# Attention over a sliding window, then a gelu layer: one pair's values and denominators in one 128-column product, and three blocks of the next first product begun ahead

## The chip, the core and the metric

The kernel runs on one core of a Trainium2 chip. A core has a matrix engine (TensorE, here PE, with its weight loads shown as PEld), a vector engine (DVE), a scalar engine for activation functions (ACT), a general engine (POOL, GpSimd) and a queue engine (SP). They run side by side and wait for each other through semaphores. DMAs are issued from SP, ACT and POOL. Matmuls write PSUM, eight banks of 512 float32 columns on 128 partitions; everything else lives in SBUF. The metric is the device time of one execution in microseconds; 311.24 us is the median of five runs before the change.

## The reference

Eight batches of 576 positions with 8 heads of 64 elements go through attention in which a position sees only those within 32 of it. The result, 4608 tokens of 512 elements, goes through a feed-forward layer with a gelu in its tanh form.

```python
scores = scale * np.matmul(q, k.transpose(0, 1, 3, 2))          # q, k, v: (8, 8, 576, 64)
mask = np.abs(pos[:, None] - pos[None, :]) <= 32
attn = softmax of the masked scores
x = np.matmul(attn, v) as (8 * 576, 8 * 64)
out = gelu_tanh(x @ w_in) @ w_out                                # (512, 2048) and (2048, 512)
```

## The kernel before

**Tiles and batches.** The feed-forward layer works on nine tiles `t` of 512 tokens. While PE does tile `t`, pieces of the attention of batch `b = t + 1` are put between its matmuls; attention writes its output, transposed and in float16, into a ring `xT` of 1536 tokens from which the next tile reads. A batch of 576 positions doesn't fit the ring evenly, so in some batches a write wraps around and becomes two instructions.

**Attention.** Heads are taken in pairs: a pair's two heads lie in the two halves of the 128 partitions. Groups 0 to 3 are the four pairs over the first 480 positions of a batch (512 in batch 0); group 4 is the rest of all pairs and is weighed in the next tile, where the plan calls it -1. A group goes through five steps. `score` (L345): matmuls of keys and queries into the two-bank tiles `S0` and `S1`, and ACT's Exp of them. `mask` (L364): DVE sets to zero what lies outside the window. `weigh` (L373): for each of four pieces of keys and each of the two heads, PE multiplies 64 columns of V by the exponentials into bank `O` (tile `ps_o`), and 64 columns of ones by the same exponentials into bank `D` (`ps_d`), which gives the denominators on 64 partitions for each head. `invert` (L398): ACT takes Ln of the denominators (L401) and Exp of minus that (L402). `spread` (L405): DVE multiplies the two and writes `xT` (L411).

**The feed-forward layer.** `ffn_in` (L429) makes a block of 128 rows of the hidden layer: four matmuls of 512 columns, one for each pair of heads (so the fourth reads what pair 3 has written), and then a gelu on ACT (L454). There are 16 blocks to a tile. The second product (`ffn_out`, L525) is done for two halves of rows and columns with seven products of sums instead of eight, each 16 matmuls of 256 columns (L544); DVE makes the sums (L490) and gathers the results, the last in `ffn_last` (L577, L582). A product accumulates in bank x0 or x1, in turns; blocks of the first product go through x0, x1 and `D`.

**What sets the order.** Each engine runs its instructions in the order in which the kernel writes them. The dictionary `PLAN` (L45) says ahead of which of the 112 matmuls of `ffn_out` a step of attention stands: `v3`, the weighing of pair 3, at 97 and `x3`, its spread, at 112, after the last. Then come `ffn_last`, and the first three matmuls of two blocks of the next tile (`begun`, L763); the next tile opens with their fourth matmuls, which wait for `x3`. ACT loads a table of functions when it goes from Exp and Ln to gelu and back (L87). After the begun blocks DVE casts the queries and keys of the next batch (`cast_and_turn`, L302), SP's queue transposes them by DMA (L313, L319), and later loads those of the batch after (`load_qk`, L152). `load_v` (L167) loads V for batches 2 to 7 from POOL's queue with five DMAs that also cast; batches 0 and 1 are loaded by SP and cast by POOL and ACT (`cast_v`, `cast_vt`).

Of the kernel before, what the change touches and what calls it, by code (L numbers as in the profile page):

```python
# [54 lines left out]
           [(t4, fc) for t4 in (2, 3) for fc in range(16)])  # L55


RING = 1536


@with_exitstack
def kernel(
# [47 lines left out]
    kinds = [MAIN[0], MAIN[1], TAIL, MAIN_0[1], TAIL_0]  # L110
    masks = [const.tile([128, width(ps)], FP16, name=f"mask{i}") for i, ps in enumerate(kinds)]
    KTs = [const.tile([128, NPAIR, 640], FP16, name=f"KT{i}") for i in range(2)]
    Vs = [const.tile([128, 5, H, 64], FP16, name=f"V{i}") for i in range(2)]
    w_in16 = big.tile([128, 4, DF], FP16, name="w_in16")
    w_out16 = big.tile([128, NF, DM], FP16, name="w_out16")
    xT = big.tile([128, NPAIR, RING], FP16, name="xT")
# [1 line left out]
    raws = {}  # L118

    def load_early(b):  # L120


        qr = rawp.tile([128, H, 256], FP32, name="qr")
        kr = rawp.tile([128, H, 256], FP32, name="kr")
        tr = tailp.tile([128, H, 64], FP32, name="tr", tag="tr")
        raws[b] = [qr, kr, tr]

        def qk(h0):
            for src, dst in ((q, qr), (k, kr)):
                nc.sync.dma_start(  # L130
                    dst[:, h0:h0 + 2, :],
                    src[b, h0:h0 + 2, 0:512, :].rearrange("h (p j) d -> p h (j d)", j=4))

        def vs(*heads):
            for h in heads:
                if h == 0:
                    raws[b].append(stage.tile([128, 4, H, 64], FP32, name="vr", tag="stage"))
                    raws[b].append(tailp.tile([128, H, 64], FP32, name="vt"))
# [116 lines left out]

    def cast_vt(b):
        n = 128 if b else 64
        (nc.gpsimd.tensor_copy if b else nc.scalar.copy)(Vs[b % 2][0:n, 4, :, :], raws[b][4][0:n])

    def cast_v(b, pr):  # L260
        vr = raws[b][3]
        hs = slice(2 * pr, 2 * pr + 2)
        nc.gpsimd.tensor_copy(Vs[b % 2][:, 0:4, hs, :], vr[:, :, hs, :])  # L263


    def cast_tails(b, eng):
        t16 = hp.tile([128, H, 64], FP16, name="t16")
        eng.tensor_copy(t16, raws[b][2])
        halfs[b].append(t16)

# [31 lines left out]
    def cast_and_turn(b):  # L302
        cast_open(b)
        q16, k16 = halfs[b]
        qr, kr, qt, kt = raws[b]
        qt16 = hp.tile([16, NPAIR, 4, 2, 64], FP16, name="qt16")
        kt16 = hp.tile([64, NPAIR, 2, 64], FP16, name="kt16")
        def queries(src, dst, p0, p1):
            for pr in range(NPAIR):
                nc.vector.tensor_copy(  # L310
                    dst[:, pr, :, :, :].rearrange("p j h d -> p h j d"),
                    src[:, 2 * pr:2 * pr + 2, :].rearrange("p h (j d) -> p h j d", j=4))
# [51 lines left out]
    def mask(b, g, hfs=(0, 1)):  # L364
        for hf, (m, prs, pieces) in enumerate(halves_of(b, g)):
            if hf not in hfs:
# [3 lines left out]
                pe, pe, m.rearrange("p (o w) -> p o w", o=1).broadcast_to(list(pe.shape)),  # L370
                op=ALU.mult)

    def weigh(b, g, other=False):  # L373

        pes = groups.pop((b, g))
# [5 lines left out]
        for i, (hf, pr, k0, c, p0, p1, off) in enumerate(todo):  # L381
            q0, n = (0, cut(b)) if g < 4 else (cut(b), 144 - cut(b))
            at = 0 if g < 4 else pr * 4 * n
            for w, bk in ((0, o), (1, d)):
                for h in range(2):
                    r0 = 64 * h
                    nc.tensor.matmul(  # L387
                        bk[r0:r0 + 64, at:at + 4 * n].rearrange(
                            "d (j p) -> d j p", j=4)[:, :, p0 - q0:p1 - q0],
                        V[:, c, 2 * pr + h, :] if w == 0 else ones,  # L390
                        pes[hf][:, h, off:off + 4 * (p1 - p0)].rearrange("k (j p) -> k j p", j=4),
                        start=(i == 0), stop=(i == len(todo) - 1), skip_group_check=True)
        return o, d
# [1 line left out]
    def size(b, g):  # L395
        return 4 * cut(b) if g < 4 else 4 * NPAIR * (144 - cut(b))

    def invert(b, g, d):  # L398
        n = size(b, g)
        lt = ap_.tile([128, 512], FP32, name="lt")  # L400
        nc.scalar.activation(lt[:, 0:n], d[:, 0:n], AF.Ln)  # L401
        nc.scalar.activation(lt[:, 0:n], lt[:, 0:n], AF.Exp, scale=-1.0)  # L402
        return lt

    def spread(b, g, o, lt):  # L405
        n = size(b, g)
        if g < 4:
            pos, done = b * S % RING, 0
            while done < n:
                e = min(n - done, RING - pos)  # L410
                nc.vector.tensor_tensor(xT[:, g, pos:pos + e], o[:, done:done + e],  # L411
                                        lt[:, done:done + e], op=ALU.mult)
                done, pos = done + e, (pos + e) % RING
        else:
            pos = (b * S + 4 * cut(b)) % RING
# [13 lines left out]
    def ffn_in(t, n, d0=0, d1=4, then=True):  # L429
# [3 lines left out]
        if d0 == 0:  # L433
            if t == 0 and 2 <= fc < 6:
                if fc % 2 == 0:
                    phs["S"] = psS.tile([128, 2, 512], FP32, name="ph2", tag=f"S{fc // 2 - 1}")
                phs[fc] = phs["S"][:, fc % 2, :]
            else:
                if t:
                    i = (first(t), 2, 1 - first(t))[n % 3] if n < NF - 1 else 2  # L440
                else:
                    i = fc if fc < 2 else (fc - 4) % 3
                phs[fc] = bank(i) if i < 2 else psO.tile([128, 512], FP32, name="ph", tag="D")
        ph = phs[fc]
        for dc in range(d0, d1):
            nc.tensor.matmul(ph, w_in16[:, dc, fc * 128:fc * 128 + 128],  # L446
# [11 lines left out]
    def first(t):  # L458

        return (t + 1) % 2  # L460

    wino = {}

# [61 lines left out]
    def ffn_out(t, i):  # L525
# [90 lines left out]

    def weighed(g):
        o, d = weigh(0, g, other=(g % 2 == 0))
        ods[g] = (o, invert(0, g, d))

    ods = {}
    score(0, 0)
# [74 lines left out]
    for t in range(NT):  # L697
        b = t + 1
        att = b < B
        if t:  # L700
            for fc in range(begun):
                ffn_in(t, fc, 3, 4)
            if att and b > 1:
                cast_and_turn(b)
            for fc in range(begun, NF):
# [11 lines left out]
        for i in range(113 if t else 65):  # L717
            for act in plan.get(i, "").split():
# [22 lines left out]
                elif kind == "v":  # L741
                    bb, gg = group(g)
                    o, d = weigh(bb, gg)
                    ods[g] = (o, invert(bb, gg, d))
# [49 lines left out]
```

## Time and profile before

| | |
|---|---|
| median of five runs | 311.24 us (310.76 to 311.39) |
| the profiled execution's own time | 311.24 us |
| its span in the profile | 309.4 us |
| PE matmuls busy | 298.1 us (96%) |
| PE weight loads busy | 187.4 us (61%) |
| DVE, ACT, POOL busy | 198.9, 199.9, 103.2 us |
| granted TensorE clock | full in all slices |
| tiles 2, 3, 5 (first matmul to first matmul of the next) | 31.81, 31.80, 31.80 us |
| tile 4 | 31.87 us |

A row of the order of time gives the start in us, the duration, the engine, the line of the kernel, the operation, output and input by the program's names, shapes, how many were merged ("x15"), and in brackets the idle time before it and what ended it. Matmuls overlap: one with 256 columns is shown as 0.27 us long, while the next starts 0.11 us later. So the pace of PE is read from the starts. "PE A <- DVE B: 0.4, 1, 0.4" in the table of waits reads: PE's A waited for DVE's B, 0.4 us in total, once, 0.4 us at the longest. The page's chain is the work that ended last, followed back to the start, as shares of the span.

### The profile page before, as it was taken

Reading aid. Unit: us, or ns where it says so; the run is one execution under the profiler, and the core shown is the slowest. Engines: PE = TensorE matmul, PEld = TensorE weight load, DVE = VectorE, ACT = ScalarE, POOL = GpSimd, SP = SyncE. Lnnn points to the kernel's source line nnn. Section 1 sums busy time; section 2 is a strip of 40 time slices with the busy share of each in tenths; the row PEclk is TensorE's granted clock in tenths of the full one; section 3 lists DMA queues with packets and bytes.
Section 4 is the critical chain, followed back from the end, with each engine's and each line's share of the span. In section 5 each row is a group of like instructions: output and inputs, shape, how many; then the busy total and the mean of one; then the engine's idle time right before and its main releaser. Section 6 shows DMA issues by size and latency. Waiting matters only on the chain.

```text
span 309.4 us, 6731 instructions
## 1 busy us (share of the span) xinstructions
PE 298.1 (96%) x2643; PEld 187.4 (61%) x2643; DVE 198.9 (64%) x453; ACT 199.9 (65%) x315; POOL 103.2 (33%) x158
## 2 busy tenths in 40 slices
PE   7879999999999999999999999999999999999993
PEld 2453545445784588548854785478647864784583
DVE  5763587868968476947784678666866643632451
ACT  1776576577677786778676776677768676706600
POOL 3656455093019110921093108510710061006000
PEclk9999999999999999999999999999999999999999
DMA  6999998999987999899779985999391022004013
GB/s 189 261 354 368 374 340 188 310 180 145 225 179 179 129 199 166 148 169 230 137 157 146 262 120 133 162 247 140 91 169 34 2 70 68 2 0 136 2 37 100
DMA packets 120061, 50.64 MB, mean 164 GB/s; under 512 B 101327, under 2 KB 113359, under 8 KB 120030
## 3 DMA queue, kind: packets, MB, share of 16 engines
q1 hardware_dynamic: 84329, 37.50, 57.7%
q0 software_dynamic: 34768, 11.54, 33.3%
q10 hardware_dynamic: 933, 1.18, 1.1%
q8 instruction: 20, 0.33, 0.5%
q14 instruction: 11, 0.09, 0.1%
HBM read 37.62 MB, written 9.44 MB: 152 GB/s over the span
## 4 chain that ended last, share of the span: by engine, by line
PE 76%; DMA 9%; SPq 7%; DVE 5%; POOL 1%; issue 1%; ACT 0%; DVEq 0%; POOLq 0%
PE mm L544 30%; PE mm L446 20%; PE ph L446 12%; PE ps_o L387 4%; DMA wst<-in_moe_w_in_dram 4%; PE ps_s L354 3%; PE ps_d L387 3%; DMA KT<-k 3%; DMA kr<-in_k_dram 2%; SPq L162 2%; PE mm L515 2%; SPq L130 2%; SPq L139 1%; POOL w_in L190 1%; SPq L181 1%
## 5 line engine op out<-in xcount | busy, mean ns | idle before, releaser
L446 PEld LDWEIGHTS <-w_in 128*128 128x128 f16 x576 | 56.0, 98 | 66.6 <-POOL w_in L190 1.7
L446 PE MATMUL mm<-xT,w_in 128*128 128x512 f16 x352 | 86.3, 379 | 0.2 <-DVE xT L411 0.2
L506 POOL DMA_DIRECT2D out_dram<-y x77 | 45.3, 595 | 115.4 <-DVE y L573 114.7
L454 ACT ACTIVATE gT<-mm 128x512 f16<-128x512 f32 x88 | 52.4, 599 | 37.2 <-PE mm L446 37.2
L446 PE MATMUL ph<-xT,w_in 128*128 128x512 f16 x224 | 58.8, 379 | 0.6 <-POOL w_in L190 0.6
L490 DVE TENSOR_TENSOR s<-gT 128x512 f16<-128x512 f16 x64 | 26.9, 420 | 42.0 <-ACT gT L454 42.0
L544 PEld LDWEIGHTS <-s 128*128 128x128 f16 x512 | 48.6, 98 | 7.5
L360 ACT ACTIVATE pe<-ps_s 128x704 f16<-128x704 f32 x64 | 43.3, 727 | 9.1 <-PE ps_s L354 8.3
L544 PE MATMUL mm<-t,s 128*128 128x256 f16 x376 | 45.7, 273 | 0.0
L401 ACT ACTIVATE lt<-ps_d 128x480 f32<-128x480 f32 (+3 forms) x40 | 22.2, 556 | 30.9 <-PE ps_d L387 30.8
L454 ACT ACTIVATE gT<-ph 128x512 f16<-128x512 f32 x56 | 33.0, 600 | 13.0 <-PE ph L446 12.9
L544 PEld LDWEIGHTS <-gT 128*128 128x128 f16 x384 | 36.0, 98 | 7.3
L369 DVE TENSOR_TENSOR pe<-pe,mask 128x704 f16<-128x704 f16 x64 | 31.8, 533 | 1.7 <-ACT pe L360 1.6
L544 PE MATMUL mm<-w_out,gT 128*128 128x256 f16 x256 | 32.8, 273 | 0.0
L411 DVE TENSOR_TENSOR xT<-ps_o,lt 128x480 f16<-128x480 f32 (+5 forms) x38 | 20.2, 549 | 12.7 <-ACT lt L402 12.7
L387 PEld LDWEIGHTS <-V 128*64 128x64 f16 x336 | 17.9, 109 | 11.3 <-issue 5.4
L402 ACT ACTIVATE lt<-lt 128x480 f32<-128x480 f32 (+3 forms) x40 | 23.5, 588 | 1.3
L387 PE MATMUL ps_o<-pe,V 128*64 128x160 f16 (+2 forms) x244 | 21.7, 241 | 1.1 <-POOL V L263 0.8
L87 ACT ACT_TABLE_LOAD x17 | 21.8, 1283 | 1.1 <-PEq L778 0.8
L387 PE MATMUL ps_d<-pe,ones 128*64 128x192 f16 (+2 forms) x264 | 22.3, 235 | 0.0
L170 POOL DMA_DIRECT2D V<-in_v_dram x24 | 22.0, 942 | 0.0
L354 PE MATMUL ps_s<-QT,KT 64*128 64x192 f16 (+5 forms) x336 | 17.9, 227 | 1.1 <-DVE KT L290 1.1
(77 smaller groups left out, 297.6 us busy)
## 6 DMA issues: line engine op xcount, KB each, us to landing
kr<-in_k_dram SPq DMA_DIRECT2D x32, 256.0 KB, 7.2
qr<-in_q_dram SPq DMA_DIRECT2D x6, 1024.0 KB, 7.5
V<-in_v_dram POOLq DMA_DIRECT2D x30, 128.0 KB, 8.1
wst<-in_moe_w_in_dram SPq DMA_DIRECT2D x3, 1024.0 KB, 8.9
wst<-in_moe_w_out_dram SPq DMA_DIRECT2D x3, 1024.0 KB
qr<-in_q_dram SPq DMA_DIRECT2D x8, 256.0 KB
vr<-in_v_dram SPq DMA_DIRECT2D x16, 128.0 KB, 7.5
out_dram<-y POOLq DMA_DIRECT2D x24, 48.0 KB, 2.4
```

What stands on the lines that cost most here:

```text
L170: nc.gpsimd.dma_start(V[:, c, :, :], v[b, :, 128 * c:128 * c + 128, :].rearrange("h p d -> p h d"))
L354: nc.tensor.matmul(ps[:, h, off:off + 4 * n].rearrange("k (j p) -> k j p", j=4), KTs[b % 2][r0:r0 + 64, pr, k0:k0 + 128], QTs[b][r0:r0 + 6 ...
L360: nc.scalar.activation(pe, ps[:, :, 0:w], AF.Exp, scale=SCALE)
L369: nc.vector.tensor_tensor(pe, pe, m.rearrange("p (o w) -> p o w", o=1).broadcast_to(list(pe.shape)), op=ALU.mult)
L387: nc.tensor.matmul(bk[r0:r0 + 64, at:at + 4 * n].rearrange("d (j p) -> d j p", j=4)[:, :, p0 - q0:p1 - q0], V[:, c, 2 * pr + h, :] if w == ...
L401: nc.scalar.activation(lt[:, 0:n], d[:, 0:n], AF.Ln)
L402: nc.scalar.activation(lt[:, 0:n], lt[:, 0:n], AF.Exp, scale=-1.0)
L446: nc.tensor.matmul(ph, w_in16[:, dc, fc * 128:fc * 128 + 128], xT[:, dc, t * 512 % RING:t * 512 % RING + 512], start=(dc == 0), stop=(dc = ...
L454: nc.scalar.activation(gTs[t][:, fc, :], phs[fc], AF.Gelu_apprx_tanh)
L490: nc.vector.tensor_tensor(dst, x, y, op=op)
L506: (eng or turn_about[0] if t == NT - 1 else eng or nc.gpsimd).dma_start(out_v[b, j, q0 + p:q0 + p + e, cols], yo[m:m + e, cols])
L544: nc.tensor.matmul(pys["apart"][:, 0:256] if apart else py[:, blk, :], lhsT, wino[w][:, f, :], start=(new and i % (8 if one else 16) == 0) ...
```

## The change

In batches 2 to 7 the weighing of pair 3 is done with 128 columns at a time. V gets a ninth place between the last two heads, filled with ones once, so that head 6 and the ones, and the ones and head 7, lie side by side. One matmul of [V6, ones] then gives in bank `O` the weighted values of head 6 on partitions 0 to 63 and its denominators on 64 to 127; one of [ones, V7] gives in bank `D` the denominators of head 7 on 0 to 63 and its values on 64 to 127. Eight matmuls with full-width weights take the place of sixteen with half-width ones. `invert` needs two Ln instructions, each on 64 partitions and from one half of the partitions to the other, and `spread` two multiplications for one, the second reading `D`. Head 7 moves to another place, so `load_v` has seven DMAs for five and the casts of the early batches are split or strided.

Three blocks of the next tile are begun ahead instead of two, the second and third in the two-bank tile `S0` of the scores. The rotation of banks in `ffn_in` and `ffn_out` is the same in every tile now and no longer swaps. Two pairs of small tiles share a buffer in SBUF (`vt` with `qt`, `t16` with `kt16`).

```diff
+FUSED = (3,)
-    Vs = [const.tile([128, 5, H, 64], FP16, name=f"V{i}") for i in range(2)]
+    Vs = [const.tile([128, 5, H + 1, 64], FP16, name=f"V{i}") for i in range(2)]
...
-        qt = tailp.tile([16, H, 256], FP32, name="qt")
+        qt = tailp.tile([16, H, 256], FP32, name="qt", tag="vt")
...
     def load_v(b):
         V = Vs[b % 2]
-        for c in range(4):
-            nc.gpsimd.dma_start(V[:, c, :, :],
-                                v[b, :, 128 * c:128 * c + 128, :].rearrange("h p d -> p h d"))
-        nc.gpsimd.dma_start(V[:, 4, :, :], v[b, :, 448:576, :].rearrange("h p d -> p h d"))
+        for c, k0 in enumerate((0, 128, 256, 384, 448)):
+            nc.gpsimd.dma_start(V[:, c, 0:7, :],
+                                v[b, 0:7, k0:k0 + 128, :].rearrange("h p d -> p h d"))
+        nc.gpsimd.dma_start(V[:, 0:4, 8, :], v[b, 7, 0:512, :].rearrange("(c p) d -> p c d", p=128))
+        nc.gpsimd.dma_start(V[:, 4, 8, :], v[b, 7, 448:576, :])
...
     def cast_vt(b):
-        (nc.gpsimd.tensor_copy if b else nc.scalar.copy)(Vs[b % 2][0:n, 4, :, :], raws[b][4][0:n])
+        copy = nc.gpsimd.tensor_copy if b else nc.scalar.copy
+        copy(Vs[b % 2][0:n, 4, 0:7, :], raws[b][4][0:n, 0:7])
+        copy(Vs[b % 2][0:n, 4, 8, :], raws[b][4][0:n, 7])
...
+    def fused(b, g):
+        return b > 1 and g in FUSED
...
+            if fused(b, g):
+                for h, bk in enumerate((o, d)):
+                    nc.tensor.matmul(
+                        bk[:, 0:4 * n].rearrange("d (j p) -> d j p", j=4)[:, :, p0:p1],
+                        V[:, c, 2 * pr + h:2 * pr + h + 2, :],
+                        pes[hf][:, h, off:off + 4 * (p1 - p0)].rearrange("k (j p) -> k j p", j=4),
+                        start=(i == 0), stop=(i == len(todo) - 1), skip_group_check=True)
+                continue
             for w, bk in ((0, o), (1, d)):
...
-        nc.scalar.activation(lt[:, 0:n], d[:, 0:n], AF.Ln)
+        if fused(b, g):
+            nc.scalar.activation(lt[0:64, 0:n], o[64:128, 0:n], AF.Ln)
+            nc.scalar.activation(lt[64:128, 0:n], d[0:64, 0:n], AF.Ln)
+        else:
+            nc.scalar.activation(lt[:, 0:n], d[:, 0:n], AF.Ln)
         nc.scalar.activation(lt[:, 0:n], lt[:, 0:n], AF.Exp, scale=-1.0)
...
-                nc.vector.tensor_tensor(xT[:, g, pos:pos + e], o[:, done:done + e],
-                                        lt[:, done:done + e], op=ALU.mult)
+                for bk, rows in ((o, slice(0, 64)), (d, slice(64, 128))) if fused(b, g) else \
+                        ((o, slice(0, 128)),):
+                    nc.vector.tensor_tensor(xT[rows, g, pos:pos + e], bk[rows, done:done + e],
+                                            lt[rows, done:done + e], op=ALU.mult)
...
-                    i = (first(t), 2, 1 - first(t))[n % 3] if n < NF - 1 else 2
+                    i = 3 if n in (1, 2) else 0 if n == 0 else (2, 1, 0)[n % 3]
...
+                if i == 3 and n == 1:
+                    phs["S"] = psS.tile([128, 2, 512], FP32, name="ph3", tag="S0")
...
-            pys[n % 2] = bank((first(t) + n) % 2)
+            pys[n % 2] = bank((1 + n) % 2)
...
             for fc in range(begun):
-                ffn_in(t, fc, 3, 4)
+                ffn_in(t, fc, 3, 4, then=False)
+            for fc in range(begun):
+                gelu(t, fc)
...
+                        if t == 1:
+                            nc.gpsimd.memset(Vs[1][:, :, 7, :], 1.0)
                         load_v(b + 1)
...
+            nc.gpsimd.memset(Vs[0][:, :, 7, :], 1.0)
             load_v(2)
...
-        begun = 2 if att else 0
+        begun = 3 if att else 0
```

More of the change, by code (lines that the diff above doesn't have):

```diff
@@ L137, in vs @@
                     raws[b].append(stage.tile([128, 4, H, 64], FP32, name="vr", tag="stage"))
-                    raws[b].append(tailp.tile([128, H, 64], FP32, name="vt"))
+                    raws[b].append(tailp.tile([128, H, 64], FP32, name="vt", tag="vt"))
                 nc.sync.dma_start(raws[b][3][:, :, h, :],
@@ L262, in cast_v @@
         hs = slice(2 * pr, 2 * pr + 2)
-        nc.gpsimd.tensor_copy(Vs[b % 2][:, 0:4, hs, :], vr[:, :, hs, :])
+        nc.gpsimd.tensor_copy(
+            Vs[b % 2][:, 0:4, 2 * pr:2 * pr + 3:2 if pr == 3 else 1, :][:, :, 0:2, :], vr[:, :, hs, :])
     def cast_tails(b, eng):
-        t16 = hp.tile([128, H, 64], FP16, name="t16")
+        t16 = hp.tile([128, H, 64], FP16, name="t16", tag="t16")
         eng.tensor_copy(t16, raws[b][2])
@@ L306, in cast_and_turn @@
         qt16 = hp.tile([16, NPAIR, 4, 2, 64], FP16, name="qt16")
-        kt16 = hp.tile([64, NPAIR, 2, 64], FP16, name="kt16")
+        kt16 = hp.tile([64, NPAIR, 2, 64], FP16, name="kt16", tag="t16")
         def queries(src, dst, p0, p1):
@@ L389, in weigh @@
                             "d (j p) -> d j p", j=4)[:, :, p0 - q0:p1 - q0],
-                        V[:, c, 2 * pr + h, :] if w == 0 else ones,
+                        V[:, c, 2 * pr + h + (pr == 3 and h), :] if w == 0 else ones,
                         pes[hf][:, h, off:off + 4 * (p1 - p0)].rearrange("k (j p) -> k j p", j=4),
@@ L396, in size, with invert, spread @@
         return 4 * cut(b) if g < 4 else 4 * NPAIR * (144 - cut(b))
-    def invert(b, g, d):
+    def invert(b, g, o, d):
         n = size(b, g)
         lt = ap_.tile([128, 512], FP32, name="lt")
-        nc.scalar.activation(lt[:, 0:n], d[:, 0:n], AF.Ln)
+        if fused(b, g):
[3 more added lines that the diff above has]
+            nc.scalar.activation(lt[:, 0:n], d[:, 0:n], AF.Ln)
         nc.scalar.activation(lt[:, 0:n], lt[:, 0:n], AF.Exp, scale=-1.0)
-        return lt
-    def spread(b, g, o, lt):
+        return lt, d
+    def spread(b, g, o, lt, d):
         n = size(b, g)
@@ L439, in ffn_in @@
                 if t:
-                    i = (first(t), 2, 1 - first(t))[n % 3] if n < NF - 1 else 2
+                    i = 3 if n in (1, 2) else 0 if n == 0 else (2, 1, 0)[n % 3]
                 else:
                     i = fc if fc < 2 else (fc - 4) % 3
-                phs[fc] = bank(i) if i < 2 else psO.tile([128, 512], FP32, name="ph", tag="D")
+                if i == 3 and n == 1:
+                    phs["S"] = psS.tile([128, 2, 512], FP32, name="ph3", tag="S0")
+                phs[fc] = bank(i) if i < 2 else phs["S"][:, n - 1, :] if i == 3 else \
+                    psO.tile([128, 512], FP32, name="ph", tag="D")
         ph = phs[fc]
@@ L456, in gelu @@
             sums(t, n // 4)
-    def first(t):
-        return (t + 1) % 2
     wino = {}
@@ L618, in weighed @@
         o, d = weigh(0, g, other=(g % 2 == 0))
-        ods[g] = (o, invert(0, g, d))
+        ods[g] = (o, *invert(0, g, o, d))
     ods = {}
@@ L743 @@
                     o, d = weigh(bb, gg)
-                    ods[g] = (o, invert(bb, gg, d))
+                    ods[g] = (o, *invert(bb, gg, o, d))
                     if t and g < 0 and b + 1 < B:
+                        if t == 1:
+                            nc.gpsimd.memset(Vs[1][:, :, 7, :], 1.0)
                         load_v(b + 1)
```

## The prediction

> **What bounds the kernel now.** I read the page first (engines, chain), then the table of who waited for whom, then the order of time around one tile's end, engine by engine.
>
> ```profile
> PE 298.1 (96%) x2643; PEld 187.4 (61%) x2643; DVE 198.9 (64%) x453; ACT 199.9 (65%) x315; POOL 103.2 (33%) x158
> PE 76%; DMA 9%; SPq 7%; DVE 5%; POOL 1%; issue 1%; ACT 0%; DVEq 0%; POOLq 0%
> ```
>
> PE is busy throughout and carries the chain; DMA and SP's queue are its opening, before the weights have come. After 60 us PE waits once (second batch's tile):
>
> ```profile
> PE ps_o L387 <- DVE xT L411: 0.4, 1, 0.4
> ```
>
> So what counts is the spacing of PE's instructions, not their busy time. Here is the end of tile 2 (PE, then DVE, then ACT, each in order of time: start, us, what):
>
> ```profile
> 121.95 0.27 PE L544 MATMUL mm<-w_out,s 128*128 128x256 f16 x1
> 122.16 0.26 PE L387 MATMUL ps_o<-pe,V 128*64 128x160 f16 x2
> 122.25 0.24 PE L387 MATMUL ps_d<-pe,ones 128*64 128x160 f16 x2
> 122.32 0.25 PE L387 MATMUL ps_o<-pe,V 128*64 128x192 f16 x2
> ...
> 122.70 0.22 PE L387 MATMUL ps_d<-pe,ones 128*64 128x128 f16 x2
> 122.86 1.81 PE L544 MATMUL mm<-w_out,s 128*128 128x256 f16 x15
> 124.51 0.81 PE L446 MATMUL mm<-xT,w_in 128*128 128x512 f16 x3
> 125.15 0.81 PE L446 MATMUL ph<-xT,w_in 128*128 128x512 f16 x3
> 125.80 0.38 PE L446 MATMUL mm<-xT,w_in 128*128 128x512 f16 x1
> ```
>
> ```profile
> 121.38 0.66 DVE L411 TENSOR_TENSOR xT<-ps_o,lt 128x480 f16<-128x480 f32 x1 [0.53 <-ACT lt L402]
> ...
> 124.21 0.66 DVE L411 TENSOR_TENSOR xT<-ps_o,lt 128x480 f16<-128x480 f32 x1 [0.90 <-ACT lt L402]
> 124.78 0.74 DVE L582 TENSOR_TENSOR y<-mm,y 128x256 f32<-128x256 f32 x2
> 125.44 1.45 DVE L310 CAST q<-qr 128x512 f16<-128x512 f32 x4
> ```
>
> ```profile
> 122.97 0.57 ACT L401 ACTIVATE lt<-ps_d 128x480 f32<-128x480 f32 x1 [0.93 <-PE ps_d L387]
> 123.57 0.60 ACT L402 ACTIVATE lt<-lt 128x480 f32<-128x480 f32 x1
> 124.19 1.28 ACT L87 ACT_TABLE_LOAD   x1
> ```
>
> The reader should see two things. The two 64-column matmuls of a "x2" row run side by side: 160 columns advance PE by 0.07 us, 192 by 0.08, 128 by 0.055. And the group pays at its edges: L544 matmuls stand 0.11 apart (15 in 1.65), yet the first L387 starts 0.21 after its forerunner, and the next L544 0.16 after the last pair instead of 0.055. Each edge costs 0.10. The six tiles that the change touches (1 to 6) show 0.90 or 0.91 from that last L544 to the next.
>
> **The change, part by part.** *The fused product (tiles 1 to 6).* Eight full-width matmuls replace eight side-by-side pairs and stream the same columns: 2 x (0.07 + 0.08 + 0.08 + 0.055), 0.58 with unrounded spacings. Nothing shows V's 128 columns loaded for a matmul this short, so the nearest row is the tail transposes, which load 128 columns for 128 moving ones:
>
> ```profile
> 55.56 0.39 PE L274 MATMUL pt<-idn,t 128*128 128x128 f16 x4
> 55.79 0.38 PE L515 MATMUL mm<-w_out,gT 128*128 128x512 f16 x1
> ```
>
> Four in 0.23, 0.056 each, no edge before or after. I take it: same width, same length. The other bound is the 0.11 spacing of the L544 stream, 8 x 0.11 = 0.88.
>
> The Trainium skill, "TensorE: Matmul & The Clock Gate", section "LDWEIGHTS (loading the stationary operand)", speaks against the change: it gives columns/1.2 ns, 107 ns for 128 columns. By that the eight loads would need 0.85, and as an estimate the six tiles would lose 0.6 us in all where I count a gain; the transposes' 0.056 decides against it here.
>
> The edge at the exit goes: 0.10. The one at the entrance goes only as far as DVE allows, since the group writes the bank that the spread of pair 2 reads. That spread ends at 121.38 + 0.66 = 122.04; DVE to PE takes 0.06 (the wait above: DVE's two rows at 83.37 end 84.08, PE starts at 84.14). So the group starts at 122.10, not 122.06. In tiles 1 and 4 the ring wraps and pair 2's spread is two instructions (0.72): it ends at 90.30 and 185.77, and entry gains nothing (90.35, 185.82 now). From last L544 to next: 0.15 + 0.58 = 0.73 in four tiles, 0.20 + 0.58 = 0.78 in two. Gain: 4 x 0.18 + 2 x 0.13 = 0.98 us.
>
> *The longer way to xT, and the third block.* Now: L401 0.57, L402 0.60, spread 0.66, end 124.87, with PE wanting xT at 125.80: 0.87 spare with the 0.06. After: the group starts at 122.10, its last matmul 0.53 later, takes 0.22, ACT starts 0.05 after (122.70 + 0.22 to 122.97): 122.90. The second Ln follows by 0.49 (gelus start at 126.22 and 126.71) and ends at 123.96; Exp to 124.59, first spread from 124.63, second 0.57 behind (124.21 to 124.78), end 125.86. No row shows half the partitions, or an ACT output on other partitions than its input; I take the full-width times, with nothing and twice as bounds. PE wants it at 122.10 + 0.58 + 1.65 + nine matmuls of 0.215 (six took 1.29) = 126.27. Spare: 0.35; 0.15 if the pairs don't overlap (0.60 and 0.66). Without the third block, 0.65 less, it would be late. The block itself adds no matmul. Its two banks of scores were last read by ACT at 122.04 (121.25 + 0.79) and are wanted from 125.16; bank 1, wanted by block 4 at 127.8, is freed by L582 at about 126.5. The table load moves to 124.6, ends 125.9, ahead of the first gelu at 126.7. The first product of each tile now always takes bank 1, last read by block 13's gelu, some 0.9 earlier. Cost nothing.
>
> *DVE later.* L582 and the casts behind it start 1.0 later (125.77 for 124.78). Behind them: the q transposes on SP's queue, then the four key transposes, then the next loads; on POOL the stores and V loads. Landing events in tile 2 put keys of pairs 1 and 2 at 108.71 and 111.96, PE wanting them at 110.20 and 113.36: spare 1.5 and 1.4, of which 1.07 goes for DVE (two split spreads precede it there) and 0.12 since PE comes earlier. Left: 0.2 to 0.3. Tile 3's least is 2.0. No cost taken; the bound is about 1 us should the landings stretch.
>
> *V loads.* Seven POOL issues for five, 2 x 0.94 = 1.9 us a tile. The last three wait for the tail group (109.01 in tile 2), after which POOL idles 13.25 us for DVE's y; first use is a tile later. The waits of these issues on earlier stores of the same queue have long been met. The two fills of ones (0.26 for 192 columns; bounds 0.2 to 0.6) delay V of batch 2 from 62.56; it is wanted at 80.43. But that traffic meets batch 2's key transposes, whose first arrival PE's weight load only just meets (0.2 waited at 75.00): -0.2 to +0.6 there, taken as 0.
>
> *The split casts.* ACT's V tail (0.61 at 12.34) becomes two instructions, up to 0.6 more, followed by 0.34 idle and hidden by the wait for w_in until 26.7; POOL's (0.62 at 52.76) is followed by 1.25 idle. SP's qt load now waits for the latter: done by 54.0 at worst, while SP reaches it at 59.74; kt stands behind it. Nothing.
>
> Sum: 311.24 - 0.98 = 310.26, against the profiled execution's own 311.24 (span 309.4, 1.8 outside); that is also the median. I say 310.3.
>
> **The rivals.** *Eaten by loads (same).* Keys or V traffic late in tiles 1 and 2 give back 0.4 to 1.2: 310.7 to 311.5. For: 0.2 to 0.3 spare is thin and DMA is at 9 tenths there. Against: V chunks carry seven heads, not eight. *Loads of weights set the pace (slower).* At 0.11 a matmul the span is 0.15 + 0.88 = 1.03 in four tiles and 1.08 in two: +0.5 + 0.35 = +0.8, 312.1. The gain is gone at 0.093 a matmul, and from 0.106 it is slower; only the transposes speak against it. *xT late (slower).* With the way to xT 0.35 + e longer than counted, PE stands e in each of six tiles; beyond e = 0.16 the gain is gone, and if each half took the full extra again (0.57 + 0.66, e = 0.9) it would be 315.6. *More (faster).* Entry gain everywhere and tile 1's 0.4 wait gone: 309.7. *The change doesn't do what it says (same).* If the full-width group has edges of 0.10 too, it lasts 0.21 + 0.58 + 0.10 = 0.89 for 0.91: 311.1. The transposes' missing edges speak against it.
>
> **How the numbers follow.** Likeliest, 309.9 to 310.6: 0.58. Eaten, or edges that stay: 0.21. Slower rivals: 0.16 together. More: 0.05. A change of 0.2%, 0.62 us, is what a measurement can tell: faster below 310.62, 0.63; same to 311.86, 0.21; slower 0.16. The range leaves out the worst of both ends: 309.7 to 311.7.
>
> **What would show it.** Right: the fused group takes 0.58, the next L544 starts 0.06 after its last matmul, tiles 2, 3, 5 and 6 last 31.62 instead of 31.80. PE waits for xT at L446's fourth slice, or idle time ended by KT in tile 2, would show the rivals; matmuls 0.11 apart in the group the weight loads. I am wrong if half-partition ACT or DVE work costs more than whole, or if landings in tile 2 stretch.

## The result, and the profile after

The changed kernel takes 311.23 us (median of 53 runs, 310.4 to 314.32); the kernel before, run beside it, 311.81 us (median of 95, 310.57 to 314.93; the 311.24 named at the start is the median of five of these). The ratio is 0.9981 with a 95% interval of 0.9972 to 0.999: a gain of about 0.6 us, at least 0.3, where the forecast's sum was 0.98 (a ratio of 0.9969, just outside the interval). The 311.23 lies inside the stated range, but 0.97 above the 310.26 of the sum: 0.57 of this is the base (311.24 in five runs, 311.81 in 95), 0.40 is gain that is missing. The forecast took 0.2% as the least that a measurement can tell; the middle of the interval, 0.19%, is just under it, and the interval reaches to both sides.

The page of the changed kernel, engines and chain, in the order of the lines shown of before:

```profile
PE 296.8 (96%) x2595; PEld 187.3 (61%) x2595; DVE 204.2 (66%) x461; ACT 201.9 (65%) x322; POOL 113.0 (37%) x173
...
PE 85%; SPq 4%; DMA 4%; DVE 3%; POOL 1%; issue 1%; ACT 0%; POOLq 0%
```

PE still carries the chain; it has 48 matmuls less (8 in each of six tiles). The table of waits has the wait of before in tile 1, and one after 60 us that is new:

```profile
PE ph L476 <- ACT gT L484: 0.7, 1, 0.7
...
PE ps_o L408 <- DVE xT L438: 0.4, 1, 0.4
```

The end of tile 2 in order of time (PE, then DVE, then ACT; start, duration, what). The lines of the code have moved: L476 is the first product (L446 before), L570 the second (L544), L399 the fused product, L423 and L424 its two Ln, L427 the Exp, L438 the spread, L484 the gelu.

```profile
121.93 0.27 PE L570 MATMUL mm<-w_out,s 128*128 128x256 f16 x1
122.07 0.23 PE L399 MATMUL ps_o<-pe,V 128*128 128x160 f16 x1
...
122.59 0.22 PE L399 MATMUL ps_d<-pe,V 128*128 128x128 f16 x1
122.64 1.80 PE L570 MATMUL mm<-w_out,s 128*128 128x256 f16 x15
124.28 0.81 PE L476 MATMUL mm<-xT,w_in 128*128 128x512 f16 x3
124.93 1.46 PE L476 MATMUL ph<-xT,w_in 128*128 128x512 f16 x6
126.22 0.38 PE L476 MATMUL mm<-xT,w_in 128*128 128x512 f16 x1
```

```profile
124.61 0.65 DVE L438 TENSOR_TENSOR xT<-ps_o,lt 64x480 f16<-64x480 f32 x1 [1.32 <-ACT lt L427]
125.29 0.66 DVE L438 TENSOR_TENSOR xT<-ps_d,lt 64x480 f16<-64x480 f32 x1
...
126.66 1.45 DVE L318 CAST q<-qr 128x512 f16<-128x512 f32 x4
```

```profile
122.79 0.57 ACT L423 ACTIVATE lt<-ps_o 64x480 f32<-64x480 f32 x1 [0.77 <-PE ps_o L399]
123.38 0.56 ACT L424 ACTIVATE lt<-ps_d 64x480 f32<-64x480 f32 x1
123.97 0.60 ACT L427 ACTIVATE lt<-lt 128x480 f32<-128x480 f32 x1
```

The group lasts 0.57 (122.07 to 122.64), and from the last L570 before it to the next there are 0.71 for 0.91 before. PE wants the finished xT at 126.22 and doesn't stand: the second spread ends at 125.95.

**Where the gain went.** A tile is measured from its first L476 (L446) to that of the next. Tiles 1 to 7 (tile 0 is the opening) took 32.27, 31.80, 31.80, 31.87, 31.80, 31.80 and 26.66 us before, and 32.22, 31.60, 31.60, 31.74, 31.60, 31.60 and 26.66 after. So 0.05, 0.20, 0.20, 0.13, 0.20 and 0.20, together 0.98: the whole forecast gain is there when the last tile begins. Then this, in the order of time of PE and of ACT:

```profile
277.49 1.03 PE L476 MATMUL mm<-xT,w_in 128*128 128x512 f16 x4
278.35 1.03 PE L476 MATMUL ph<-xT,w_in 128*128 128x512 f16 x4
280.06 1.89 PE L476 MATMUL ph<-xT,w_in 128*128 128x512 f16 x8 [0.69 <-ACT gT L484]
```

```profile
278.55 0.60 ACT L484 ACTIVATE gT<-mm 128x512 f16<-128x512 f32 x1 [9.46 <-PE mm L476]
279.41 0.60 ACT L484 ACTIVATE gT<-ph 128x512 f16<-128x512 f32 x1 [0.27 <-PE ph L476]
```

and the same place of the kernel before:

```profile
278.45 1.03 PE L446 MATMUL mm<-xT,w_in 128*128 128x512 f16 x4
279.31 1.03 PE L446 MATMUL ph<-xT,w_in 128*128 128x512 f16 x4
280.17 1.89 PE L446 MATMUL mm<-xT,w_in 128*128 128x512 f16 x8
```

Before, a block starts every 0.86. After, block 2 starts 1.71 behind block 1, 0.85 late, and only when block 1's gelu (279.41 + 0.60) is done. Blocks 1 and 2 lie in the two halves of `S0`, the buffer (a tile of PSUM, in the kernel's word) that otherwise holds scores. In tiles 1 to 7 all three first blocks are begun ahead and their gelus are written behind all of them. Tile 8 isn't begun ahead (`begun` is 0 once no attention is left), so each block's gelu stands behind it in the order of writing, and block 2's matmuls, which write the buffer that the gelu reads, wait for it, though the two use different halves. The first two experiments test this.

A second measure is needed for what follows, since the opening (before tile 1) differs by 1.3 us between two profiles of the changed kernel, and by 2 us among all twelve profiles, as the last section shows. From the first matmul of tile 1 to the end of the span the kernel before takes 248.99 us, the changed one 248.75, and 248.75 again in a second profile. In this measure the change is worth 0.24: 0.98, less 0.85 between the first matmul of tile 8 and the start of the last one of the second product (26.78 for 25.93), plus 0.10 gained behind that, in the stores (4.94 for 5.05). The 0.10 needn't be the change's: all the other kernels show 4.93 to 5.00 there, and of the kernel before there is one profile only.

### The profile page after: what moved, and what is told of

Its sections match the earlier page's. It is cut to its first block, busy times and chain, and to the rows that moved or that the text cites. A ratio compares the mean times of both kernels' runs of the same rounds, so it can differ in the third digit from the quotient of the medians.

```text
span 309.2 us, 6674 instructions
## 1 busy us (share of the span) xinstructions
PE 296.8 (96%) x2595; PEld 187.3 (61%) x2595; DVE 204.2 (66%) x461; ACT 201.9 (65%) x322; POOL 113.0 (37%) x173
## 4 chain that ended last, share of the span: by engine, by line
PE 85%; SPq 4%; DMA 4%; DVE 3%; POOL 1%; issue 1%; ACT 0%; POOLq 0%
PE mm L570 30%; PE mm L476 21%; PE ph L476 16%; PE mm L541 5%; PE ps_s L362 4%; PE ps_o L408 4%; DMA wst<-in_moe_w_in_dram 4%; PE ps_d L408 2%; SPq L134 2%; SPq L143 1%; POOL w_in L195 1%; SPq L186 1%; PE ps_o L399 1%; DVE t L506 1%; PE py L570 1%
## 5 line engine op out<-in xcount | busy, mean ns | idle before, releaser
L476 PEld LDWEIGHTS <-w_in 128*128 128x128 f16 x576 | 56.0, 98 | 67.3 <-POOL w_in L195 1.6
L476 PE MATMUL mm<-xT,w_in 128*128 128x512 f16 x320 | 78.0, 379 | 0.1
L484 ACT ACTIVATE gT<-mm 128x512 f16<-128x512 f32 x80 | 47.6, 599 | 36.3 <-PE mm L476 35.6
L476 PE MATMUL ph<-xT,w_in 128*128 128x512 f16 x256 | 64.6, 379 | 1.2 <-ACT gT L484 0.7
L570 PEld LDWEIGHTS <-s 128*128 128x128 f16 x512 | 48.8, 98 | 7.0
L570 PE MATMUL mm<-t,s 128*128 128x256 f16 x376 | 45.8, 273 | 0.0
L484 ACT ACTIVATE gT<-ph 128x512 f16<-128x512 f32 x64 | 36.3, 602 | 12.3 <-PE ph L476 12.1
L570 PEld LDWEIGHTS <-gT 128*128 128x128 f16 x384 | 36.0, 98 | 7.4
L174 POOL DMA_DIRECT2D V<-in_v_dram x30 | 29.1, 984 | 22.8 <-PE ps_d L408 14.3
L426 ACT ACTIVATE lt<-ps_d 128x480 f32<-128x480 f32 (+3 forms) x34 | 18.8, 553 | 25.3 <-PE ps_d L408 25.2
L570 PE MATMUL mm<-w_out,gT 128*128 128x256 f16 x256 | 32.8, 273 | 0.0
L438 DVE TENSOR_TENSOR xT<-ps_o,lt 128x480 f16<-128x480 f32 (+10 forms) x38 | 20.3, 548 | 15.9 <-ACT lt L427 15.7
L427 ACT ACTIVATE lt<-lt 128x480 f32<-128x480 f32 (+3 forms) x40 | 23.5, 587 | 1.3
L408 PEld LDWEIGHTS <-V 128*64 128x64 f16 x288 | 15.4, 109 | 9.9 <-issue 4.4
L408 PE MATMUL ps_o<-pe,V 128*64 128x160 f16 (+2 forms) x196 | 17.5, 241 | 1.0 <-DVE pe L377 0.4
L408 PE MATMUL ps_d<-pe,ones 128*64 128x160 f16 (+2 forms) x216 | 18.2, 234 | 0.0
```

The source lines that it names most:

```text
L174: nc.gpsimd.dma_start(V[:, c, 0:7, :], v[b, 0:7, k0:k0 + 128, :].rearrange("h p d -> p h d"))
L408: nc.tensor.matmul(bk[r0:r0 + 64, at:at + 4 * n].rearrange("d (j p) -> d j p", j=4)[:, :, p0 - q0:p1 - q0], V[:, c, 2 * pr + h + (pr == 3 ...
L570: nc.tensor.matmul(pys["apart"][:, 0:256] if apart else py[:, blk, :], lhsT, wino[w][:, f, :], start=(new and i % (8 if one else 16) == 0) ...
```

## The experiments

Ten runs were made of nine kernels (the changed one once more, and one of the others twice), in three groups, each group on one chip beside the kernel before. "Tile 1 to end" is the measure just named, from one profile of each run.

| kernel | ratio to before, 95% interval | tile 1 to end, us | against before |
|---|---|---|---|
| before | 1 | 248.99 | |
| changed | 0.9981 (0.9972 to 0.999) | 248.75 | -0.24 |
| changed, once more | 0.9986 (0.9966 to 1.0007) | 248.75 | -0.24 |
| own tile for block 2 in the last tile | 0.9959 (0.9937 to 0.9981) | 247.92 | -1.07 |
| last tile begun ahead | 0.9957 (0.9935 to 0.9979) | 247.94 | -1.05 |
| the same once more | 0.9953 (0.9938 to 0.9969) | 247.91 | -1.08 |
| third block alone | 1.0029 (1.0008 to 1.005) | 249.74 | +0.75 |
| fused product alone | 1.0208 (1.0174 to 1.0242) | 255.09 | +6.10 |
| two begun, both in S tiles | 1.0017 (0.9999 to 1.0035) | 249.81 | +0.82 |
| pair 3 four matmuls later | 1.0004 (0.9979 to 1.003) | 249.26 | +0.27 |
| last tile ahead, pair 2 two earlier | 1.0003 (0.9984 to 1.0021) | 249.55 | +0.56 |
| last tile ahead, pair 2 one earlier, pair 3 one later | 0.9952 (0.9936 to 0.9967) | 247.53 | -1.46 |

**The wait of the last tile taken away, in two ways.**

```diff
+                if i == 3 and n == 2 and t == NT - 1:
+                    phs["S"] = psS.tile([128, 2, 512], FP32, name="ph4", tag="S1")
```

> Only the second of the two blocks that share the scores' tile S0 in the last tile of the feed-forward layer is put into S1. Theory A (the fused product brings 0.98 us, as forecast, and 0.85 of it is lost in the last tile, where PE waits for the gelu of the block before because the two blocks lie in one tile): the wait of 0.69 us at 280.06 goes, the periods of tiles 1 to 7 stay as in the changed kernel, the last tile is 0.85 shorter, and the time is 0.98 below the kernel before, a ratio of 0.9969. Rival B (the missing part of the gain is noise of the opening of the run or is lost after the last product, in the stores): the wait goes but the end does not move, and the ratio stays at 0.998. Rival C (the gelus are the bound of the last tile's opening, so the wait only moves on): a new wait for ACT of the same size appears at one of the next three blocks, ratio 0.998.

The order of time of this kernel, PE, at the place of the wait:

```profile
279.07 1.03 PE L478 MATMUL mm<-xT,w_in 128*128 128x512 f16 x4
279.93 2.75 PE L478 MATMUL ph<-xT,w_in 128*128 128x512 f16 x12
```

Twelve matmuls in a row, no wait. All periods are those of the changed kernel, and from tile 1 to the end there are 0.83 less. Theory A holds; B and C, by which the end would not have moved, fall. The other way:

```diff
-        begun = 3 if att else 0
+        begun = 3 if t < NT - 1 else 0
```

> The last tile is begun three blocks ahead like the others, so that no gelu stands between the two blocks in S0. Theory A: the wait in the last tile goes, the time is the same as with the separate bank, ratio 0.9969. Rival C (gelus too slow for the opening of the last tile): three gelus start 0.6 later than in the run with the separate bank, and PE waits for ACT at block 4 or 5, 0.2 to 0.6, ratio 0.998.

0.81 less, again with no wait. What the two have in common is only that the gelu no longer stands between two blocks of one tile.

**The third block alone.**

```diff
-FUSED = (3,)
+FUSED = ()
```

> The third block and the rotation of banks stay, the product of pair 3 goes back to 64 columns. Theory A: the span between the two products at the end of tiles 1 to 6 is 0.90 again, the periods are those of the kernel before within 0.03, and the wait of the last tile is still there: 0.85 slower than before, ratio 1.0027, and 0.98 slower than the changed kernel. Rival D (the third block itself brings part of the gain, by covering the way to xT): the periods are below those of before, 31.80, by 0.05 or more. Rival B: ratio 1.000, as the wait in the last tile costs nothing at the end.

The periods are 32.27, 31.80, 31.80, 31.87, 31.80 and 31.80, to the hundredth those of before, and the span between the products is 0.91 in all six tiles. The wait is there too:

```profile
282.13 1.89 PE L476 MATMUL ph<-xT,w_in 128*128 128x512 f16 x8 [0.69 <-ACT gT L484]
```

So in tiles 1 to 7 the third block and the new rotation bring nothing by themselves and cost nothing; all of the 0.98 is the product's, all of the 0.85 is the rotation's, and the two add. (From tile 1 to the end it is 0.75, since this kernel's stores are 0.1 shorter too.) Rivals B and D fall.

**The fused product alone**, with two blocks begun and the rotation of before:

```diff
-                    i = 3 if n in (1, 2) else 0 if n == 0 else (2, 1, 0)[n % 3]
+                    i = (first(t), 2, 1 - first(t))[n % 3] if n < NF - 1 else 2
...
-            pys[n % 2] = bank((1 + n) % 2)
+            pys[n % 2] = bank((first(t) + n) % 2)
...
-        begun = 3 if att else 0
+        begun = 2 if att else 0
```

> The fused product stays, two blocks are begun ahead as in the kernel before, with its rotation of banks. xT is then wanted 0.65 earlier. Theory E (the way to xT is longer than forecast, so that only 0.2 of spare were left with three blocks): PE waits 0.43 to 0.45 for DVE at the opening of each of the tiles 2 to 7, 2.6 in all, against 0.98 gained, and nothing in the last tile: 1.6 slower than before, ratio 1.0052. As forecast (0.35 of spare): waits of 0.30, 1.8 in all, 0.8 slower, ratio 1.0026. If the third block was not needed: no wait, ratio 0.9969.

All three expectations are missed: 6.1 slower, not 1.6. The waits, the end of tile 2 on PE, and then on DVE:

```profile
PE ph L476 <- DVE xT L438: 6.1, 6, 1.2
```

```profile
126.15 0.81 PE L476 MATMUL mm<-xT,w_in 128*128 128x512 f16 x3
127.88 0.82 PE L476 MATMUL ph<-xT,w_in 128*128 128x512 f16 x3 [0.92 <-DVE xT L438]
```

```profile
126.48 0.65 DVE L438 TENSOR_TENSOR xT<-ps_o,lt 64x480 f16<-64x480 f32 x1 [1.32 <-ACT lt L427]
127.16 0.66 DVE L438 TENSOR_TENSOR xT<-ps_d,lt 64x480 f16<-64x480 f32 x1
```

It isn't the fourth matmul (which reads xT) that stands, but the *first* of block 1, a block that reads nothing of pair 3 yet. In the old rotation block 1 opens in bank `D`. Before, `D` held only denominators and was free once Ln had read it; now it holds head 7's values as well and is free only when the second spread has read it (127.16 + 0.66). By their starts, the first matmuls of the block are 1.08 late in four tiles and 1.40 in two (the table of waits counts from the modelled end of the matmul before, and so has 0.92 for 1.08): 7.1, less the 0.98, gives the 6.1. That the table's sum is 6.1 too is chance. So the third block's bank is not only there to give the way to xT more time: the new rotation keeps the tile's opening out of `D`. The next run parts the two causes.

**Two blocks begun, both in tiles of the scores.**

```diff
-                if i == 3 and n == 1:
-                    phs["S"] = psS.tile([128, 2, 512], FP32, name="ph3", tag="S0")
-                phs[fc] = bank(i) if i < 2 else phs["S"][:, n - 1, :] if i == 3 else \
+                if i == 3:
+                    phs["S"] = psS.tile([128, 2, 512], FP32, name="ph3", tag=f"S{n - 1}")
+                phs[fc] = bank(i) if i < 2 else phs["S"][:, 0, :] if i == 3 else \
...
-        begun = 3 if att else 0
+        begun = 2 if att else 0
```

> Two blocks are begun ahead instead of three, with the changed kernel's rotation, but blocks 1 and 2 of every tile each have a tile of the scores of their own, so that no block opens in the bank D and none waits for a gelu in S0. Theory H (in the run with the product alone, the second block waited for bank D, which the fused product's second spread now reads, and that cost 1.1 to 1.4 a tile; the way to xT alone costs 0.65 less the spare of 0.2): PE waits about 0.45 for DVE in each of six tiles, 2.7 in all, now at the first block's fourth matmul, 250.6 us from the first matmul of tile 1 to the end. As forecast (spare 0.35): 0.30 each, 249.7 us. Rival (the long waits of that run were the way to xT after all): 1.1 to 1.4 a tile again, 255 us.

```profile
126.39 0.81 PE L476 MATMUL ph<-xT,w_in 128*128 128x512 f16 x3
127.47 0.38 PE L476 MATMUL mm<-xT,w_in 128*128 128x512 f16 x1 [0.26 <-DVE xT L438]
```

The wait has moved to the fourth matmul and is 0.43 (127.47 less 126.39 is 1.08; three matmuls at 0.215 would be 0.65) after tiles 2, 3, 5 and 6. After tile 1 it is 0.23 and after tile 4 there is none, so the sum is 1.95, and 249.81 is 1.89 above the 247.92 of the kernel without waits. Theory H has the size right, 0.45, but not the number of tiles. The sum alone would fit the forecast's 249.7; what decides is the wait in each tile, 0.43 and not 0.30. In batches 2 and 5 the ring wraps and the spread is four instructions, of which the next tile reads only what the first two write (384 and 192 columns): there xT is early. The spare time is thus 0.65 less 0.43, 0.22, in four tiles. Of the 1.08 lost in each of them in the run with the product alone, the way to xT explains 0.43; the bank is the rest.

**The spare time from the other side.**

```diff
-        61: "v1 s3", 64: "x1", 80: "m3", 81: "v2 s4", 88: "x2", 97: "v3", 104: "m4", 112: "x3"}
+        61: "v1 s3", 64: "x1", 80: "m3", 81: "v2 s4", 88: "x2", 101: "v3", 104: "m4", 112: "x3"}
```

> In the changed kernel the weighing of pair 3 stands four matmuls later, which takes 0.44 from the spare time of xT. Theory E (0.2 of spare, since the halves of Ln and of the spread follow each other by 0.59 and 0.68): PE waits 0.24 for DVE at the fourth matmul of the opening of six tiles, 1.45 in all; the entrance of the fused product is free and gains 0.4; in all 1.0 slower than the changed kernel, 249.8 us from the first matmul of tile 1 to the end. As forecast (0.35 of spare): waits of 0.09, 0.55 in all, 248.9 us. No wait at all would show that the spare is more than 0.44.

```profile
124.32 1.46 PE L476 MATMUL ph<-xT,w_in 128*128 128x512 f16 x6
125.83 0.38 PE L476 MATMUL mm<-xT,w_in 128*128 128x512 f16 x1
```

Six matmuls at 0.215 are 1.29; the fourth slice comes after 1.51, so PE stands 0.22 (by the row before, whose matmuls are shown to run until 125.78, it would be only 0.05: starts tell it, ends are modelled). 0.44 less 0.22 is a spare of 0.22 again. It stands in the same four tiles, not in six: 4 x 0.22 lost, 0.37 gained at the entrances, 0.51 above the changed kernel. That is neither expectation's sum (1.0 and 0.15); with Theory E's wait and four tiles it is 0.88 - 0.37. The entrance, with the spread of pair 2 long done, lasts 0.11 in all six tiles, and the whole span between the products 0.69.

**An attempt at a faster version, with the entrance freed.**

```diff
-        61: "v1 s3", 64: "x1", 80: "m3", 81: "v2 s4", 88: "x2", 97: "v3", 104: "m4", 112: "x3"}
+        61: "v1 s3", 64: "x1", 79: "v2", 80: "m3", 81: "s4", 88: "x2", 97: "v3", 104: "m4", 112: "x3"}
...
-        begun = 3 if att else 0
+        begun = 3 if t < NT - 1 else 0
```

> The last tile is begun three blocks ahead, and the weighing of pair 2 stands two matmuls earlier, so that its spread is done 0.2 earlier. Theory F (the fused product's entrance is held by that spread alone): the span between the two products falls from 0.87 to 0.68 in tile 1, from 0.79 to 0.68 in tile 4 and from 0.71 to 0.68 in the others, 0.4 in all; with the 0.85 of the last tile, 1.25 below the changed kernel, 247.5 us from the first matmul of tile 1 to the end, ratio to the kernel before 0.995. Rival G (the weight load of a fused product costs its exposed time after any wait or none): tile 1 and 4 stay at 0.87 and 0.79, 247.9 us, ratio 0.9965.

Both miss: 249.55, 1.6 above the kernel with the last tile begun ahead. In tile 2 on PE and on DVE:

```profile
119.99 0.22 PE L408 MATMUL ps_d<-pe,ones 128*64 128x128 f16 x2
120.15 0.28 PE L570 MATMUL mm<-t,s 128*128 128x256 f16 x1
120.27 0.27 PE L570 MATMUL mm<-t,gT 128*128 128x256 f16 x1
120.47 0.34 PE L362 MATMUL ps_s<-QT,KT 64*128 64x96 f16 x8
```

```profile
120.47 0.69 DVE L593 TENSOR_TENSOR y<-mm,y 128x512 f32<-128x512 f32 x1 [1.30 <-PE mm L570]
121.08 0.92 DVE L377 TENSOR_TENSOR pe<-pe,mask 128x704 f16<-128x704 f16 x2
121.91 0.65 DVE L438 TENSOR_TENSOR xT<-ps_o,lt 128x480 f16<-128x480 f32 x1
```

Pair 2's weighing and the scores of group 4 stood side by side; now two matmuls of the second product stand between them, and each border costs: 0.10 a tile. And the first of these two is the last of a product, which DVE gathers at L593. With the weighing ahead of it that row starts later, the masks behind it too, and the spread starts at 121.91 though its Exp was done at 121.46. The spread that was to be earlier is later, and the spans between the products are 0.95, 0.89, 0.81, 0.88, 0.81 and 0.81, 0.65 more than the changed kernel's 4.50 in all. With six borders at 0.10 and 0.33 more at a wait of the scores for a key transpose in tile 1 (75.19), that is 1.58 of the 1.61. The 0.33 stands ahead of the first place that this run changed, so it is a difference between executions, and not its doing.

**The same aim, with both neighbours kept together and behind the product's end.**

```diff
-        61: "v1 s3", 64: "x1", 80: "m3", 81: "v2 s4", 88: "x2", 97: "v3", 104: "m4", 112: "x3"}
+        61: "v1 s3", 64: "x1", 80: "m3 v2 s4", 88: "x2", 98: "v3", 104: "m4", 112: "x3"}
...
-        begun = 3 if att else 0
+        begun = 3 if t < NT - 1 else 0
```

> The last tile is begun three blocks ahead; the weighing of pair 2 and the scores of group 4 stand together one matmul earlier, after the end of a product, and the weighing of pair 3 one later. Theory F2 (the entrance of the fused product is held by the spread of pair 2; the run with pair 2 two matmuls earlier lost because it cut pair 2 off from the scores of group 4, which adds two edges of 0.1 a tile, and pushed the end of a product behind it, which made DVE's spread later rather than earlier): the span between the products is 0.69 or less in all six tiles, the periods are 31.57 to 31.59 in tiles 2, 3, 5 and 6, 31.63 in tile 4, 32.04 in tile 1; of the spare of 0.22 for xT 0.11 is left and PE waits for nothing at the openings; from the first matmul of tile 1 to the end 247.57 us, 0.37 less than with the last tile begun alone, ratio to the kernel before 0.9955. Rival G (entrances stay as they are whatever the spread does): 247.94 us.

```profile
122.26 0.38 PE L570 MATMUL mm<-w_out,s 128*128 128x256 f16 x2
122.47 0.23 PE L399 MATMUL ps_o<-pe,V 128*128 128x160 f16 x1
...
123.06 1.69 PE L570 MATMUL mm<-w_out,s 128*128 128x256 f16 x14
...
125.23 1.46 PE L476 MATMUL ph<-xT,w_in 128*128 128x512 f16 x6
126.53 0.38 PE L476 MATMUL mm<-xT,w_in 128*128 128x512 f16 x1
```

The span between the products is 0.69 in all six tiles, the periods are 32.04, 31.57, 31.57, 31.64, 31.57 and 31.57, PE doesn't stand at the openings, and from tile 1 to the end it takes 247.53, where 247.57 was expected. It beats the kernel before by 0.5% (310.35 for 311.83) and the changed one by 1.22 in the traces. The kernel with the last tile begun ahead ran beside it:

> The changed kernel with the last tile begun three blocks ahead, once more, beside the run above on the same chip: 247.94 us from the first matmul of tile 1 to the end, ratio to the kernel before 0.9957 to 0.997.

247.91 and a ratio of 0.9953. The times of the two (310.35 and 310.23) don't tell them apart; that the one with the freed entrance is 0.38 shorter rests on the traces alone.

The changed kernel itself ran beside the second group:

> The changed kernel as it is, beside the following runs. All theories: the period of tiles 2, 3, 5 and 6 is 31.60, PE waits 0.69 for ACT in the last tile, and from the first matmul of tile 1 to the end of the span there are 248.75 us; the ratio lies between 0.997 and 0.9995.

Its periods, its wait and its 248.75 came out the same. This second ratio, 0.9986, doesn't exclude no change by itself.

## Why the prediction was right in part and wrong in its size

**The step that failed** is "The block itself adds no matmul ... Cost nothing." It was worked out for the tiles that are begun ahead: who read the two banks of the scores last, and when they are wanted. Tile 8, where `begun` is 0 and the same line of code gives blocks 1 and 2 the two halves of one tile with a gelu between them, was left out. The cost there is 0.85 in the trace, and 0.83 and 0.81 came back when it was taken away. The kernel without it comes out 1.07 below before (ratios of 0.9959, 0.9957 and 0.9953 against the forecast's 0.9969, which lies inside two of the three intervals and at the edge of the third). No rival named this wait either. "Eaten by loads" had the right band of times, 310.7 to 311.5, by luck: in tile 2 the keys of pairs 1 and 2 landed at 109.07 and 111.80, 1.1 and 1.5 ahead of the scores that read them (110.17 and 113.34), where 0.2 to 0.3 was feared. PE's wait wasn't at loads but at a bank.

**The fused product.** Its sum, 0.98, is what the periods show; that it agrees to the hundredth is luck, by two sizes that were off against each other. The group took 0.57 to 0.59 for 0.58, the exit 0.05, and the four unwrapped tiles 0.71 for a forecast 0.73: 4 x 0.20 instead of 4 x 0.18. Tile 4 came to 0.79 for 0.78. Tile 1 gained 0.05 instead of 0.13: the spread ended at 90.32 and the product started at 90.47, 0.15 later, not the 0.06 that tiles 2 and 4 show. That pair 2's spread holds the entrance is shown by the runs that took it away: 0.69 in every tile, tile 1 among them. Where the 0.09 more of tile 1 lie, the weight loads show, in the order of time in tiles 1 and 2, and then by line (count, shortest, median and longest in ns, first and last start):

```profile
90.44 0.60 PEld L399 LDWEIGHTS <-V 128*128 128x128 f16 x8 [0.27 <-issue]
...
121.93 0.70 PEld L399 LDWEIGHTS <-V 128*128 128x128 f16 x8
```

```profile
L399 PEldq EVENT_SEMAPHORE  x1: 51/51/51, 90.4 to 90.4; - x1
```

In tile 2 the first load stands ahead of the end of the spread (121.36 + 0.66). In tile 1 it comes 0.12 behind it, after an instruction that only waits, 51 ns long (for DVE; the load itself then waits for POOL), and tile 1 alone has one. In the run with pair 2 two matmuls earlier tiles 1 and 2 have one, and in both the group starts 0.15 behind the spread, against 0.06 in the other four. These two are the groups that first read each of the two buffers of V after POOL has filled in the ones; that this is why they wait twice is likely, but no run tests it.

The rival by which loads of weights set the pace fell: matmuls followed each other by 0.055 to 0.085, never by 0.11. The group of the fused product's weight loads in the changed kernel, with the count, then busy time in us, mean ns of one, and idle time before it:

```profile
L399 PEld LDWEIGHTS <-V 128*128 128x128 f16 x48 | 3.8, 97 | 0.7 <-issue 0.3 <-DVE xT L438 0.2
```

48 loads of 97 ns would be 4.66 one after the other, and are 3.8: in this group they overlap each other. The Trainium skill, "TensorE: Matmul & The Clock Gate", section "LDWEIGHTS (loading the stationary operand)", gives columns/1.2 ns, which is 107 ns for 128 columns. The length of one load in this trace is near that, but taken as the distance from one to the next it would have made the eight 0.85, and the trace has 0.57.

**The way to xT.** The halves were priced as whole rows, rightly (Ln 0.57 and 0.56, spread 0.65 and 0.66 on 64 partitions), but they follow each other by 0.59 and 0.68, not by the 0.49 and 0.57 borrowed from gelus and from a spread with another operation behind it. So the spare was near its lower bound, 0.22 by two runs, instead of 0.35 (bounds 0.15 and 0.35). It was enough. (The forecast says that no row of before shows half the partitions. Some did: DVE's cast of 64x512, L323, took 405 ns on average, its cast of 128x512, L310, 424. They spoke for whole-row prices.) "Without the third block, 0.65 less, it would be late" was right, but was less than half of the reason: without the new rotation bank `D` costs 1.1 a tile (1.4 where the ring wraps). That the second spread reads `D` was known; the forecast did not ask who opens there.

**The rest.** DVE's casts came 1.22 later (126.66 for 125.44), not 1.0, and nobody waited. The two fills of ones took 0.53 and 0.39 on POOL, inside the bounds of 0.2 to 0.6; V's traffic made no wait. ACT's split cast took 0.56 and 0.25 for 0.61, in the opening, where nothing can be told to 0.1.

**What stays open.** The medians give the change 0.6 (0.3 to 0.9), the part from tile 1 on only 0.24. The difference would lie in the opening, but there the profiles differ by more than that among themselves, so it isn't shown. In nine of the eleven rows of the table the times (the ratio times the median of before) are 0.04 to 0.5 us better than the traces from tile 1 on, in two 0.15 and 0.4 worse. The rows share their runs of the kernel before. So an opening that is some tenths shorter is possible, but no run tests it.

## What to carry to other kernels

A rule that picks buffers by block number has to be followed through every tile, the first and last above all: where a tile opens differently (here without blocks begun ahead), two blocks that share a tile get a reader between them. Before values are put in a buffer that used to be read early, look for everyone who opens in it next: its release moves to the latest reader. And a piece of work did best here when it was moved together with its neighbours and behind the end of a product, not ahead of it; each new border cost 0.10, and the row that gathers the product was held up as well.

## What the hardware showed that wasn't expected

- Work on half of the partitions took as long as on all: Ln 0.57 and 0.56 on 64x480 for 0.57 on 128x480, a spread 0.65 and 0.66 for 0.66. Two such halves don't overlap either: spreads from different banks and to different partitions start 0.68 apart.
- The opening of the program isn't the same twice. The first matmul of tile 1 stood at 60.04, 60.29, 60.31, 60.43, 60.46, 60.85, 60.93, 60.97, 61.55, 61.70, 61.80 and 62.05 in the twelve profiles, the changed kernel's own at 60.46 and 61.80, while from there to the end its two profiles agree within 0.01, and those of the kernel with the last tile begun ahead within 0.03. For changes under 1 us the profile from that point tells more than the time of a run, as long as no wait for a DMA differs behind it, as the 0.33 in one run did.
